# Attention and feed-forward on one core: attention steps of the last two blocks taken in pairs, weights and kept sums stored as pairs of parts

## The chip, the core and the metric

The kernel runs on one core of a Trainium2 chip. The metric is the device time of one execution in microseconds (us). A core has TensorE (PE in the rows; its weight loads are PEld), VectorE (DVE), ScalarE (ACT), GpSimd (POOL), and SyncE (SP), which here issues nearly all DMAs.

## What is computed

Windowed causal attention over 8 batches of 8 heads, 576 tokens, head size 64, then a feed-forward layer with a piecewise gate on all 4608 tokens:

```python
scores = scale * np.matmul(q, k.transpose(0, 1, 3, 2))
mask = (rel >= 0) & (rel < 64)                    # rel = query position - key position
attn = softmax(np.where(mask, scores, -1e9))
x = (attn @ v).transpose(0, 2, 1, 3).reshape(4608, 512)
h = x @ w_in                                      # 512 -> 2048
g = np.where(h >= 1, h, np.where(h <= -1, 0.0, (h + 1) ** 2 / 4))
out = g @ w_out                                   # 2048 -> 512
```

## The kernel before, in words

**Tiling.** Attention goes in 36 steps of 128 tokens, all heads in one step. A step has a scores part (`att_scores`: 64 matmul records of 96 columns for nearly all steps, S in what follows) and a values part (`att_values`: 32 records of 64 columns, V). The feed-forward layer works on tiles of 512 tokens with matmuls of 128x512. Every float32 operand of it is split into a high and a low part, and a product is three matmuls: high by high, high by low, low by high. I call the feed-forward matmuls dense.

**Stages.** Three tiles of 512 tokens go plainly (`add_ffn`, lines 1139 and 1185). The other six go as three blocks of 1024 tokens (`add_super`), in which seven products of halves take the place of eight. Its sums of weights are made once (`add_sums`) and kept in DRAM (`kept`); each group of 6 dense matmuls then reads one part of them through a ring of 7 buffers (`add_ring`, `ring_load`). The first layer of a block is line 914 (`ffn_product`), the second line 1000 (`out_product`). The attention of a block has 8 steps and runs inside the dense work of the block before it.

**Order.** No queue is filled by hand. Each piece of work is added to a list with a key, a cost for each engine that may do it, and what it waits for, takes and gives (`Plan.add`). `Plan.run` goes through the list with these costs, the free buffers and the keys, and writes each engine's instructions in the order in which it took them. The constants at the top (`A_SUPER`, `B_DUE`, `W_LATE`, ...) shift the keys or are costs. On the chip each engine then takes its instructions in that order, and waits on semaphores.

**One step from scores to values** (steps from 5 on): S into two banks of PSUM (`ps_a`); on DVE `att_masked` (line 445, 8 instructions of 128x96), on ACT `att_exp` (line 465, 8 activations), on DVE `att_inverse`, on DVE or POOL `att_normalize` (line 484), on DVE `att_turn` (line 491, a transpose in squares of 32). Then SP writes the result to a DRAM tile in two DMAs (`att_write`, `moved<-sm`) and reads it back transposed (`att_read`, `ptd<-moved`). There is one such DRAM tile and one buffer for the read (`pt2=1`), so a write waits for the read before it, and a read for the V that uses the buffer. V is followed by `x_take`, a copy out of PSUM on ACT or DVE (`raw<-ps_a`).

In the blocks `add_step` holds two steps open (`BEHIND = 2`). Each of the middle six steps gives PE one item: V of an older step, then S of the new one. The first two steps of a block are lone S, the last two V lone:

```python
            def do(e):
                if t < PLAIN:
                    att_scores(s, masked, ps)
                att_values(sv, pj)
                if t >= PLAIN:
                    att_scores(s, masked, ps)
```

**Start.** The first four steps add the mask by a matmul (line 415) and transpose on PE (`att_transpose_pe`, line 520), since the way over DRAM takes longer. Meanwhile the weights are loaded as 64-bit numbers (`raw<-in_w`) and made into high and low parts on ACT and DVE (`w_rest`, `w_top`, `w_join`, `w_high`, `w_low`; lines 328 to 344).

Of the kernel before, what the change touches and what calls it, by code (L numbers as in the profile page):

```python
# [10 lines left out]
F32 = mybir.dt.float32  # L11
# [9 lines left out]
P = 128  # L21
# [21 lines left out]
E_SPAN = 5.91  # L43
E_LEAD = 17.1
W_LEAD = -23.43
W_FIRST = (41.07, 11.15, 26.87, -10.88, -31.72)
W_STEP = 25.17
L_LEAD = -2.38
W_LATE = (3.63, -16.39, 9.21, 20.15, 0.56)
V_LATE = 14.51  # L50
W0_KEY = -103.61
FIRST_LOAD = 0, (0,)
M_LATE = 5.76
W0_STEP = 8.68
FINE = 4
NWARM = 8
A_FIRST = (-100.35, -96.85, -96.18, -80.14)
A_NEXT = 10.78
A_STEP = 5.01
A_SPAN = 18.65  # L60
A_LEAD = 5.32
O_LAG = 2.91
# [11 lines left out]
B_DUE = (4.53, -27.23, 1.18)  # L74
B_STEP = 13.93
B_FIRST = -15.42
A_END = 2.75
V_PE = 1270
NORM = dict(Pool=800, DVE=480), dict(DVE=610)
G_LATE = (11.92, 0.97, -5.01, 12.64, 1.72)  # L80
D_LATE = (-2.36, 0.62, 26.98, 2.89, 13.75, 21.44)
TURN = 965, 1500
# [4 lines left out]
SUM_KEEP = 880  # L87
V_LATE_2 = 43.01
LAND = 800
WRITE = 1140  # L90
BACKLOG = 2500
MOVED = 3700
PATIENCE = dict(ACT=300, DVE=0, Pool=303, PE=0, SP=0)
BUFS = dict(qt=2, kt=2, vt=4, ps_a=2, sm=2, ptd=3, pt2=1, x=2, u=2, ps_h=2, a=2, gh=2, gl=2, acc=4, o=2, tmp=2)
BUFS.update({n: 1 for n in ("xtmp", "xs0", "xs1", "xs2", "xs3", "xs4", "xs5", "X", "Y")}, raw=4, ring=7, op=5)

# [4 lines left out]
S_LATE = 5.22  # L101
S_PACE = 47.29
O_CHANGE = (-1.18, 7.84, 12.31)
EARLY_2 = 3.64
A_SUPER = ((10.49, 4.41), (12.01, 4.44))
A_ORDER = (0, 4, 1, 5, 2, 6, 3, 7)
BUILD = (-17.42, 29.27)
# [5 lines left out]
R_LEAD = -10.33  # L113
R_LOAD = 370
L_DVE = 4, 6, 8
G_LEAD = (9.32, -1.73, 0.08, 4.82)
OP_LEAD = 45.65
D_LEAD = 1.02
# [6 lines left out]
class Plan:  # L125
# [29 lines left out]
    def run(self):  # L155
# [22 lines left out]
        for _ in self.work:  # L178
            best = None
            for e in engines:  # L180
# [12 lines left out]
                if could:  # L193
                    until = min(could)[0] + PATIENCE[e]
                    c = min((c for c in could if c[0] <= until), key=lambda c: c[1:])
                    best = c if best is None else min(best, c)
# [26 lines left out]
def banded_attention_then_ffn(ctx: ExitStack, tc: tile.TileContext, q, k, v, w, masks, out, out_t, dims):  # L223
# [26 lines left out]
    idt = const.tile([P, P], F32, name="idt")  # L250
    make_identity(nc, idt)
    msk = const.tile([P, 3, WIN], F32, name="msk")
# [51 lines left out]
    ws, wts, zs, us = {}, {}, {}, {}  # L304
# [29 lines left out]
    def w_high(g, eng):  # L334
        f, units = g
        ws[g] = t = wpool.tile([P, len(units), 2, DM], F32R, name="wts", tag=f"w{f}_{units[0]}")
        for j, u in enumerate(units):
            wts[f, u] = t[:, j]
        us[g] = us[g].bitcast(F32).rearrange("p (u n) -> p u n", n=DM)
        copy(eng, t[:, :, 0], us[g])  # L340

    def w_low(g):
# [1070 lines left out]
```

## Time and profile before

| | |
|---|---|
| median of 3 runs | 836.71 us (836.44 to 837.24) |
| profiled execution | 835.11 us, its span 833.2 us |
| PE busy | 817.4 us, 98% of the span |
| DVE, ACT, POOL busy | 673.7, 520.8, 229.8 us |
| moved by DMA | 216.06 MB, 259 GB/s on the mean |

The span goes from the first instruction to the last. PE's busy time is the union of its matmuls, whose ends are modelled; where the text needs what a part really takes, it uses the distance from the start of one row to the start of the next. "[0.58 <-DMA ptd<-moved]" at the end of a row says that the engine sat idle for 0.58 us before it and what ended that.

### The profile page before, as it was taken

How to read it: one execution, taken by the hardware profiler on the slowest of the kernel's cores; microseconds unless marked ns; L12 is line 12 of the kernel's file. 1: busy time of each engine (PE TensorE's matmuls, PEld its weight loads, DVE VectorE, ACT ScalarE, POOL GpSimd, SP SyncE). 2: the span in 40 equal slices, each digit the busy share in tenths (PEclk: the TensorE clock that was granted, in tenths of full speed). 3: DMA queues.
4: the chain of work that ended last, by engine and by line, in shares of the span. 5: the costliest groups of instructions: out<-in, count | busy, mean ns of one | idle time of the engine just before them, and what ended most of it. 6: DMA issues, size and time to landing. Idle time of an engine off the chain costs nothing.

```text
span 833.2 us, 18542 instructions
## 1 busy us (share of the span) xinstructions
PE 817.4 (98%) x6588; PEld 670.0 (80%) x6588; DVE 673.7 (81%) x1551; ACT 520.8 (63%) x1287; POOL 229.8 (28%) x244
## 2 busy tenths in 40 slices
PE   5999999999999999999999999999999999999998
PEld 4778888888887888888888788888888888888886
DVE  6999976467765699599899995888999948888964
ACT  7889955555666656667875563777655535566442
POOL 1000043346645744556223321140133101100100
PEclk8999999999999999999999999999999999999999
DMA  9993389976778985899978979899787786666675
GB/s 350 421 418 107 103 273 358 358 241 207 220 254 267 286 258 159 285 313 341 332 221 278 311 240 341 276 293 311 221 240 230 251 252 193 193 194 194 202 218 162
DMA packets 151900, 216.06 MB, mean 259 GB/s; under 512 B 11905, under 2 KB 75265, under 8 KB 151809
## 3 DMA queue, kind: packets, MB, share of 16 engines
q1 hardware_dynamic: 151520, 213.97, 79.6%
q8 instruction: 52, 0.85, 0.4%
q10 hardware_dynamic: 288, 0.92, 0.3%
q14 instruction: 40, 0.32, 0.1%
HBM read 163.72 MB, written 51.12 MB: 258 GB/s over the span
## 4 chain that ended last, share of the span: by engine, by line
PE 87%; DMA 6%; DVE 5%; ACT 1%; issue 0%; SPq 0%; ACTq 0%; DVEq 0%
PE acc L1000 23%; PE acc L1185 14%; PE ps_h L1139 14%; PE ps_h L914 14%; PE acc L914 14%; PE ps_a L422 3%; DMA kt<-in_k 2%; PE ps_h L535 1%; PE acc L535 1%; PE ps_a L535 1%; DMA vt<-in_v 1%; DMA ptd<-moved 1%; DVE g L978 1%; DVE op L991 1%; DMA raw<-in_w 1%; DMA moved<-sm 1%
## 5 line engine op out<-in xcount | busy, mean ns | idle before, releaser
L1000 PE MATMUL acc<-op,wts 128*128 128x512 f32 x576 | 138.4, 391 | 0.0
L294 ACT CAST op<-g 128x512 fp32r<-128x512 f32 x125 | 77.7, 622 | 84.4 <-PE acc L1000 49.3
L1139 PE MATMUL ps_h<-xh,wts 128*128 128x512 f32 (+1 forms) x424 | 129.9, 373 | 0.0
L1000 PEld LDWEIGHTS acc<-op,wts 128*128 128x128 f32 x576 | 107.6, 188 | 22.9
L1185 PE MATMUL acc<-wts,gh 128*128 128x512 f32 x384 | 120.3, 395 | 0.0
L991 DVE TENSOR_TENSOR op<-g,op 128x512 fp32r<-128x512 f32 x119 | 87.6, 737 | 17.7 <-ACT op L294 17.0
L465 ACT ACTIVATE sm<-sm,nm 128x96 f32<-128x96 f32 x248 | 89.5, 363 | 14.3 <-DVE nm L445 12.5
L914 PE MATMUL ps_h<-wts 128*128 128x512 f32 x360 | 92.1, 391 | 0.0
L914 PE MATMUL acc<-wts 128*128 128x512 f32 x360 | 91.9, 390 | 0.0
L1139 PEld LDWEIGHTS ps_h<-xh,wts 128*128 128x128 f32 x424 | 77.5, 188 | 15.2 <-issue 0.3
L1185 PEld LDWEIGHTS acc<-wts,gh 128*128 128x128 f32 x384 | 70.7, 188 | 15.4
L1154 ACT ACTIVATE a<-a 128x512 f32<-128x512 f32 (+1 forms) x129 | 79.5, 617 | 3.9
L914 PEld LDWEIGHTS acc<-wts 128*128 128x128 f32 x360 | 67.4, 188 | 14.6 <-issue 0.3
L914 PEld LDWEIGHTS ps_h<-wts 128*128 128x128 f32 x360 | 67.2, 188 | 14.6
L1139 PE MATMUL ps_h<-xl,wts 128*128 128x512 f32 (+1 forms) x212 | 78.6, 371 | 0.0
L1185 PE MATMUL acc<-wts,gl 128*128 128x512 f32 x192 | 74.9, 390 | 0.0
L1149 ACT ACTIVATE a<-g 128x512 f32<-128x512 f32 x96 | 60.3, 629 | 19.9 <-DVE g L929 15.1
L1161 DVE SCALAR_TENSOR_TENSOR g<-a,g 128x512 f32<-128x512 f32 x96 | 67.9, 714 | 5.4 <-ACT a L1154 5.2
L1171 POOL TENSOR_TENSOR gl<-a,gh 128x512 fp32r<-128x512 f32 (+1 forms) x34 | 46.8, 1378 | 59.8 <-ACT gh L1166 55.0
L1149 ACT ACTIVATE a<-ps_h 128x512 f32<-128x512 f32 (+1 forms) x53 | 29.5, 557 | 53.4 <-PE ps_h L1139 53.0
L1161 DVE SCALAR_TENSOR_TENSOR a<-a,ps_h 128x512 f32<-128x512 f32 (+1 forms) x53 | 33.6, 634 | 34.8 <-ACT a L1154 34.5
L978 DVE TENSOR_TENSOR g<-g 128x512 f32<-128x512 f32 x82 | 56.9, 708 | 0.4
(142 smaller groups left out, 1529.4 us busy)
## 6 DMA issues: line engine op xcount, KB each, us to landing
wts<-kept SPq DMA_DIRECT2D x240, 256.0 KB, 3.5
vt<-in_v SPq DMA_DIRECT2D x72, 256.0 KB, 5.7
ptd<-moved SPq DMA_DIRECT2D x31, 512.0 KB, 4.6
kt<-in_k SPq DMA_DIRECT2D x35, 384.0 KB, 6.0
kept<-wts SPq DMA_DIRECT2D x48, 256.0 KB, 4.6
gh<-kept SPq DMA_DIRECT2D x48, 256.0 KB, 3.5
gl<-kept SPq DMA_DIRECT2D x48, 256.0 KB, 3.7
raw<-in_w SPq DMA_DIRECT2D x12, 1023.8 KB, 12.3
```

The costliest lines, as they stand in the source:

```text
L294: nc.scalar.copy(dst, src)
L465: nc.scalar.activation(t, t, AF.Exp, bias=nm[:, g:g + 1], scale=-1.0, accum_out=den[:, g:g + 1])
L914: nc.tensor.matmul(ps, lhsT=r[:, part, cp], rhs=x_op(k, xp)[:, cp], start=j in (0, 1, 3, 4) and i == 0 and cp == 0, stop=j in (1, 2, 5, 6) ...
L978: engine[eng].tensor_tensor(out=g[:, out], in0=g[:, a], in1=g[:, b], op=op)
L991: engine[eng].tensor_tensor(out=low, in0=g_of(n)[:, of], in1=high.bitcast(F32), op=ALU.subtract)
L1000: nc.tensor.matmul(opened[b][m], lhsT=r[:, part, m], rhs=op[xp], start=j in (0, 1, 3, 4) and i == 0 and n == 0, stop=j in (1, 2, 5, 6) and ...
L1139: nc.tensor.matmul(ps, lhsT=wts[f, 0][:, part, c * P:(c + 1) * P], rhs=x[:, c, r], start=(c == 0 and j == 0), stop=(c == NP - 1 and j == 2),)
L1149: nc.scalar.activation(gs[t, f, r.start][0], phs[t, f, r.start], AF.Relu, bias=0.5, scale=0.5)
L1154: nc.scalar.activation(a, a, AF.Square)
L1161: nc.vector.scalar_tensor_tensor(out=ps if t >= PLAIN else a, in0=a, scalar=1.0, in1=ps, op0=ALU.min, op1=ALU.max)
L1171: engine[eng].tensor_tensor(out=g[2], in0=g[0], in1=g[1].bitcast(F32), op=ALU.subtract)
L1185: nc.tensor.matmul(acc[t, i][:, n], lhsT=g[:, sub], rhs=wts[f, 1][:, part, n], start=(q == 0 and j == 0), stop=(q == NF - 1 and j == 2 and ...
```

## The change

1. **Pairs of steps.** In the last two blocks `add_pairs` takes the place of `add_step`. A block's 8 steps make 4 pairs and 5 runs on PE: S S, three times V V S S, V V. The first S of a pair takes two banks of `acc` or `ps_h`, the second two of `ps_a`, which it gets when both V before it have been copied out. A table `P_SHIFT` shifts each run, by the change's words so that borders of PE's instruction packets fall well.
2. **Two buffers for the read** (`pt2=2`): the old one, and two tiles in the room of the early masks and of `lent`, which was the ring's fifth buffer. The ring has 6 buffers instead of 7. The write still waits for the read before it, since the DRAM tile is still one.
3. **Weights as pairs of parts.** Weights lie as [chunk of 128][high, low][128] instead of [high, low][512]. Kept sums go to DRAM in one DMA of 1 KB packets where there were two of 512 B; the second layer's plain matmuls read their moving operand in 4 pieces of 128.
4. **POOL may do more**: `w_low`, the early `att_normalize`, and `ffn_low` of the first tile.
5. **Fewer waits in the plan**: the sums of `x_sums` and `g_sum` wait only for what they read.
6. **10 more matmul records in the warm-up**, and new values of nearly all constants, so that the order moves everywhere.

```diff
-TURN = 965, 1500
+TURN = 965, 100
-V_LATE_2 = 43.01
+V_LATE_2 = 63.45
+P_SHIFT = ((-0.59, -6.76, -5.83, 5.27, -24.12), (2, 5.54, 6, 4.47, -26.37))
...
+    def turned_of(b):
+        if b == 0:
+            return [turned[:, i] for i in range(2)]
+        if not spare:
+            spare.extend(const.tile([P, NP * SB], F32, name="ptd", tag=m) for m in ("lent", "early"))
+        return spare
...
-        x = add(key - W_LATE[4], dict(DVE=low), lambda e: w_low(g), [x], gives=[("u", xr)])
+        x = add(key - W_LATE[4], dict(DVE=low, Pool=200 + 2.15 * m), lambda e: w_low(g, e), [x], gives=[("u", xr)], shared=True)
...
+    def add_turn(s, xs, dk, banks, sm):
...
+        x = [add(due, dict(SP=HOP_SP[0]), lambda e, j=j: att_write(s, j), [x, *last["d"]], moves=packets(192, 1024, WRITE), gives=[sm] * j) for j in range(2)]
+        x = add(due, dict(SP=HOP_SP[1]), lambda e: att_read(s, x), x + last["t"] + early_values, takes=["pt2"], moves=packets(256, 2048))
+        last["d"] = last["t"] = [x]
+        return x
...
+    def add_pairs(u):
...
+            for j, (s, xt_, v) in enumerate(before):
+                after = [xs] if j else needs + [y for _, a, b in before for y in (a, *b)]
+                xs = add(
+                    now if j else key, dict(PE=V_RUN[j] + (150 if r == 4 and j else 0)), lambda e, s=s: att_values(s, "ps_a"), after,
+                    takes=["ps_a"] + room * (j == 0), gives=[("pt2", xt_), ("vt", v[0]), ("vt", v[1])],
+                )
...
+            x1 = add(
+                now if before else key, dict(PE=S_RUN[not before]), lambda e, s=steps[0], pj=pj: att_scores(s, False, pj), [xs] if before else needs,
+                takes=[] if before else room, gives=[("qt", q), ("kt", k)],
+            )
...
+            x2 = add(
+                now, dict(PE=S_RUN[2]), lambda e, s=steps[1]: att_scores(s, False, "ps_a"), [x1], takes=["ps_a", "ps_a"],
+                gives=[("qt", q), ("kt", k)],
+            )
...
     for u in range(SUPERS):
-        for i in A_ORDER:
-            add_step(PLAIN + 2 * u, i)
+        if u:
+            add_pairs(u)
+        else:
+            for i in A_ORDER:
+                add_step(PLAIN, i)
         add_super(u)
```

**What moves on PE, in the first layer of the first block** (L535 and L422 are V and S before, L564 and L435 after; L914 and L999 dense; a record count in the trace is twice the count of V and S here). Before:

```order
L914 MATMUL ps_h<-wts 128x512 x6
L535 MATMUL acc<-ptd,vt 64x64 x16
L422 MATMUL ps_a<-kt,qt 32x96 x32
L914 MATMUL acc<-wts 128x512 x6
L914 MATMUL ps_h<-wts 128x512 x6
L914 MATMUL acc<-wts 128x512 x6
L914 MATMUL ps_h<-wts,gh 128x512 x6
L914 MATMUL acc<-wts,gl 128x512 x6
L535 MATMUL acc<-ptd,vt 64x64 x16
L422 MATMUL ps_a<-kt,qt 32x96 x32
```

After:

```order
L999 MATMUL acc<-wts 128x512 x6
L564 MATMUL ps_a<-ptd,vt 64x64 x32
L435 MATMUL acc<-kt,qt 32x96 x32
L435 MATMUL ps_a<-kt,qt 32x96 x32
L999 MATMUL ps_h<-wts 128x512 x6
```

Two V and two S stand in one run. In the last two blocks 10 runs each become 5. Between the runs now stand 120, 108, 246 and 126 dense matmuls in the first of these blocks' attention, and 168, 186, 156 and 108 in the second's.

**On POOL at the start**, after the masks are made. Before:

```order
L273 MEMSET msk 64x64 x2
L494 MEMSET ptd 64x256
L828 TENSOR_TENSOR u<-wts 128x256 x2
L835 TENSOR_TENSOR u<-u 128x128 x4
```

After:

```order
L284 MEMSET early 64x64 x2
L357 TENSOR_TENSOR wts<-u,wts 128x4x128
L497 TENSOR_TENSOR sm<-sm,den 128x512 x3
L357 TENSOR_TENSOR wts<-u,wts 128x4x128
L497 TENSOR_TENSOR sm<-sm,den 128x512
L1256 TENSOR_TENSOR gl<-a,gh 128x256 x2
L357 TENSOR_TENSOR wts<-u,wts 128x8x128
L1256 TENSOR_TENSOR gl<-a,gh 128x256
L497 TENSOR_TENSOR sm<-sm,den 128x768
```

POOL takes 7 of the 20 weight subtractions (2 of 512, 5 of 1024 columns) and 5 of the 10 early normalizations, which DVE did.

**On SP, around a pair** of the second block's attention, in the change:

```order
L515 DMA moved<-sm 64x3x256 x2
L979 DMA gh<-kept_92 128x512
L979 DMA gl<-kept_93 128x512
L979 DMA wts<-kept_94 128x512
L533 DMA ptd<-moved 128x512 x2
L979 DMA wts<-kept_95 128x512
L979 DMA wts<-kept_94 128x512
L979 DMA wts<-kept_95 128x512
L515 DMA moved<-sm 64x3x256 x2
```

The second step's write stands behind the first step's read, with ring loads between them.

## Rows read from the trace of the kernel before

**Rows 1.** The page, DMA queues, PE's instructions: packets, MB, share of 16 engines.
```profile
q8 instruction: 52, 0.85, 0.4%
```

**Rows 2.** Busy time by stretch: length, PE, PEld, DVE, ACT, POOL, clock, DMA share, GB/s.
```profile
20.90:25.75 4.85, 4.85 (x106) 3.71 (x105) 4.78 (x11) 3.73 (x10) 0.00 (x0) 1.00 1.04 425
...
60.00:100.00 40.00, 40.00 (x293) 32.66 (x293) 38.93 (x67) 37.36 (x74) 0.30 (x1) 1.00 0.36 122
...
330.00:830.00 500.00, 498.99 (x3455) 409.59 (x3453) 421.19 (x883) 298.34 (x676) 113.24 (x99) 1.00 0.81 255
```

**Rows 3.** Waits of PE: who for whom, us in total, times, longest.
```profile
PE ps_a L422 <- DMA qt<-in_q: 2.2, 1, 2.2
...
PE ps_h L535 <- DMA ptd<-moved: 0.8, 1, 0.8
...
PE ps_a L535 <- DMA ptd<-moved: 0.6, 1, 0.6
```

**Rows 4.** Timeline of PE around a V with an S: start, length, instruction.
```profile
342.18 1.52 PE L914 MATMUL ps_h<-wts 128*128 128x512 f32 x6
343.63 1.15 PE L535 MATMUL acc<-ptd,vt 128*64 128x64 f32 x32
344.71 1.00 PE L422 MATMUL ps_a<-kt,qt 64*32 64x96 f32 x64
345.63 1.67 PE L914 MATMUL acc<-wts,gh 128*128 128x512 f32 x6
347.14 1.55 PE L914 MATMUL ps_h<-wts,gl 128*128 128x512 f32 x6
```

**Rows 5.** The same in the second layer: dense work after an S, then a lone V.
```profile
453.69 1.67 PE L1000 MATMUL acc<-op,gl 128*128 128x512 f32 x6
...
460.44 0.39 PE L1000 MATMUL acc<-gh,wts 128*128 128x512 f32 x1
460.76 1.15 PE L535 MATMUL ps_a<-ptd,vt 128*64 128x64 f32 x32
461.84 1.66 PE L1000 MATMUL acc<-op,wts 128*128 128x512 f32 x6
463.33 1.52 PE L1000 MATMUL acc<-op,gh 128*128 128x512 f32 x6
464.69 1.52 PE L1000 MATMUL acc<-op,gl 128*128 128x512 f32 x6
```

**Rows 6.** The same at the start.
```profile
1.46 3.78 PE L284 MATMUL acc<-ptd 128*128 128x128 f32 x16 [1.46 <-DVE ptd L278]
...
22.97 1.15 PE L535 MATMUL acc<-ptd,vt 128*64 128x64 f32 x32
24.05 0.73 PE L415 MATMUL acc<-mskr,idr 128*128 128x512 f32 x2
...
31.34 0.63 PE L520 MATMUL ps_a<-idt,sm 128*128 128x128 f32 x4 [0.58 <-DVE sm L484]
...
51.12 1.10 PE L422 MATMUL ps_a<-kt,qt 64*64 64x128 f32 x32 [0.46 <-DMA kt<-in_k]
```

**Rows 7.** Timeline of ACT: the copy out of PSUM after the lone V.
```profile
461.96 0.59 ACT L294 COPY raw<-ps_a 128x512 f32<-128x512 f32 x1 [0.42 <-PE ps_a L535]
```

**Rows 8.** Chain of waits, 440 to 485 us: turn, (write,) read, V.
```profile
467.94 0.89 DVE sm L491
...
472.45 5.08 DMA ptd<-moved
477.67 1.15 PE ps_a L535 x32
```

**Rows 9.** Groups by line and shape, 330 to 650 us: busy, mean ns, idle before.
```profile
L465 ACT ACTIVATE sm<-sm,nm 128x96 f32<-128x96 f32 x119 | 43.0, 363 | 9.1 <-DVE nm L445 8.5 <-POOL sm L484 0.6
```

**Rows 10.** DVE from 10 to 100 us, by line: busy, mean ns.
```profile
L344 DVE TENSOR_TENSOR wts<-u,wts 128x1024 fp32r<-128x1024 f32 (+1 forms) x17 | 17.1, 1013 | 0.4 <-ACT wts L294 0.4
...
L484 DVE TENSOR_TENSOR sm<-sm,den 128x512 f32<-128x512 f32 (+1 forms) x12 | 8.6, 728 | 0.0
```

More of the change, by code (lines that the diff above doesn't have):

```diff
@@ L630, in add_build @@
         i0 = add(due, tt(2 * SB), lambda e: x_sums(r, 0, e), [x0, x1], takes=["xtmp"] + ["u"] * first, shared=True)
-        xs = i0
-        for j in range(1, 4):
-            xs = add(due, tt(2 * SB), lambda e, j=j: x_sums(r, j, e), [xs], shared=True)
-        end = []
+        i2 = add(due, tt(2 * SB), lambda e: x_sums(r, 1, e), [i0], shared=True)
+        i1 = add(due, tt(2 * SB), lambda e: x_sums(r, 2, e), [i0], shared=True)
+        i3 = add(due, tt(2 * SB), lambda e: x_sums(r, 3, e), [i1], shared=True)
+        lows = []
         for k in range(6):
             n = 4 * SB if k == 0 else 2 * SB
-            after, slot, takes = [xs], f"xs{k}", []
+            after, slot, takes = [(i0, i1), (i2,), (i3,), (x0, x1), (x0, x1), (x0, x1)][k], f"xs{k}", []
+            after = list(after)
             if (u, k) in x_of:
@@ new lines, in add_loads @@
+    def add_loads(s, lk, vk, vc):
+        xq = add(lk, dict(SP=390), lambda e: load_q(s), takes=["qt"], moves=packets(P, 4 * DM))
+        xk = add(lk, dict(SP=480), lambda e: load_k(s) if s else None, takes=["kt"], moves=packets(P, 6 * DM) if s else None)
+        xv = add(vk, dict(SP=vc), lambda e: load_v(s, 0), takes=["vt"], moves=packets(P, 4 * DM), behind=last["v"])
+        xw = add(vk, dict(SP=vc), lambda e: load_v(s, 1), takes=["vt"], moves=packets(P, 4 * DM), behind=[xv])
+        last["v"] = [xw]
+        return xq, xk, xv, xw
@@ new lines, in add_take @@
+    def add_take(u, i, due, xo, pv):
+        s, r = starts[PLAIN + 2 * u] // SB + i, i % 4
+        after, takes = [xo], []
+        if i < 4:
+            takes = ["raw"]
+            if u == 0:
+                after.append(x_in[PLAIN - 2])
+        else:
+            after.append(raw_of[u, r])
+        x = add(due, dict(ACT=485, DVE=608), lambda e: x_take(s, i, e), after, takes=takes, gives=[(pv, xo)])
+        if i < 4:
+            raw_of[u, r] = x
+        else:
+            add_build(u, r, max(due, 0), raw_of[u, r], x)
@@ L1252, in add_gate @@
         xl = add(
-            key + late[4], low, lambda e: ffn_low(t, f, r, e), [xh], takes=["gl"], gives=[("a", xa)], shared=t > 0,
+            key + late[4], low, lambda e: ffn_low(t, f, r, e), [xh], takes=["gl"], gives=[("a", xa)], shared=True,
         )
```

301 lines of the change are left out of this document (167 added, 134 removed).

## Prediction

> **What bounds the kernel now.** Start with the table of stretches: from 330 to 830 us PE is busy for 498.99 of 500 us, and from 60 to 100 for all 40, at the full clock [rows 2]. So what other engines do there costs nothing as long as PE doesn't wait, and it hardly does: the waits of PE on the read after the turn are 0.8 and 0.6 us, once each, and the largest shown, 2.2, is that for the first queries [rows 3]. A time can fall in three ways: PE's own instructions take less, PE starts sooner, or these few waits go.
>
> Does PE work at full rate while busy? A group of 6 dense matmuls takes 464.69 - 463.33 = 1.36 us, 0.227 each [rows 5]. Around attention it is slower. Take a V with an S [rows 4] from start to start: the 6 ahead of it take 343.63 - 342.18 = 1.45 (0.09 over 1.36), V 1.08, S 0.92, the 6 behind 1.51 (0.15 over). So a run has **edges** of 0.24 us beside V and S. Around a lone V [rows 5] the matmul ahead takes 0.32 (0.09 over 0.227) and the 6 behind 1.49 (0.13 over): edges of 0.22. That is what pairs can save.
>
> **The change, part by part** (gain positive).
>
> *Fewer runs.* Each of the two blocks has 6 runs of V and S, 2 lone S, 2 lone V. With 0.24 for a run that ends in S and 0.22 for one that ends in V that is 8 x 0.24 + 2 x 0.22 = 2.36 us a block. After, it is 4 x 0.24 + 0.22 = 1.18. **Gain 2.4** for both. Elsewhere there are 29 runs where there were 28: **-0.2**.
>
> *Joints inside a run.* There will be 8 joints of V with V and 8 of S with S; no row has one. Below: V takes 1.08 us ahead of S [rows 4] and ahead of dense work [rows 5] alike, so it may take 1.08 ahead of V, and the joint gains 0. Above: a joint may save all that stands behind a part at an edge, 0.13 for V, 0.15 for S: 8 x 0.28 = 2.2. I take half, since V and S use the array in other shapes than dense work and have none to change at such a joint: **1.1**.
>
> *Second S waits for banks.* It needs the banks of both V, so the copy of the second must end while the first S (0.92 us) runs. After the lone V, which ended at 461.84, the copy ended at 461.96 + 0.59 = 462.55, 0.71 later [rows 5, 7]: in time. At worst another copy of 0.59 is ahead of it, and it is 0.4 late, or 0.6 behind something longer: 0 to 0.6, six times. I take 0.1: **-0.6** (0 to -3.6).
>
> *Old waits on the read.* 0.8 and 0.6 [rows 3]. With two buffers a read needn't wait for the V before; pairs move the later one. **1.2** (0 to 1.4).
>
> *New waits on the read.* The costliest unknown. The write of a pair's second step must wait until the read of the first has landed (SP's order: write, read, write). What a turn, write and read take is seen once where V waited for them: 477.67 - 467.94 = 9.73 us, of which the turn 0.89 and the read's landing 5.08 [rows 8]. Two in sequence, the second turn being done by then: 9.73 + 8.84 = 18.6 us. Ahead of this lie masks, exponentials, normalization, in DVE's queue. In the traced step S ended at 453.69 [rows 5] and the turn began at 467.94, 14.3 us later, behind other DVE work. The change orders fewer instructions ahead of most turns; what must be there needs about 5 (an estimate: 8 exponentials at 0.363 are 2.9 [rows 9]; a normalization of 768 columns by that of 512, 0.73 [rows 10], is 1.1; a mask and two short ones make up the rest). So from a run's end to the second V's data it is between 24 and 33 us. Available are the dense matmuls up to the run and its first V: 120, 108, 246, 126, 168, 186, 156, 108 at 0.227, plus 1.08: 28.3, 25.6, 56.9, 29.7, 39.2, 43.2, 36.4, 25.6. At 26.6 the two shortest are late by 1.0 each: **-2.0**, which I take as near the low end, since these turns have been given early places. At 24 it is 0; at 33 it is 4.7 + 7.4 + 3.3 + 7.4 = 22.8.
>
> *Start.* DVE is busy for 38.9 of 40 us from 60 to 100, POOL for 0.3, and for nothing in the earlier stretch shown [rows 2]. Moving 5 normalizations at 0.73 and 7 weight subtractions at 1.01 (means over both lengths) takes 10.7 us off DVE [rows 10]. PE's waits that hang on it: 0.58 in the third transpose, as an example; and 0.46 on keys, whose load now stands ahead of most weights on SP [rows 6]. That is 1.0 us shown, and I take **1.5**, as the 10.7 us lie on the engine that PE's first work waits for (3.5 if dense work also starts a third of them sooner, -2.5 if it starts later, since the third scores and the second V now stand ahead of it). The 10 more warm-up records, 3.78 / 16 = 0.24 each [rows 6], are 2.4 us, nearly inside the 2.2 us wait for the first queries [rows 3]: 0; if queries came at once, -2.4.
>
> *At nothing:* moving operands in 4 pieces. An early V reads 64 columns in a row, a later one 2 pieces of 32; 22.97 to 24.05 and 343.63 to 344.71 are 1.08 each [rows 4, 6]. Fewer, larger DMA packets of kept sums: no wait of PE on them is listed. One ring buffer less: 6 groups of 1.36 are 8.2 us ahead, and SP's issues keep their place; with that cover gone PE would wait at each group, which I hold for unlikely.
>
> **Sum:** 2.4 - 0.2 + 1.1 - 0.6 + 1.2 - 2.0 + 1.5 = **3.4 us**. The profiled execution of 835.11 (span 833.2, and 1.9 around it) would become 831.7. The median of the runs shown stands 1.6 above it, 836.71; from there I forecast **833.3**.
>
> **A rule to weigh: PE's instruction packets.** The queue for PE's instructions moved 52 packets of together 0.85 MB, 16 KB each; 0.4% of 16 engines' 833 us over 52 is 1.03 us a packet [rows 1]. An S issues its 64 matmuls with as many weight loads in 0.92 us [rows 4], so 256 instructions would last 1.84 us, longer than a packet's transfer. In before no V or S around a border is longer than the others. The Trainium skill (Runtime: NRT & Kernel Launch, Instruction fetch mechanics) says that instructions are fetched in blocks of 256 while the block before runs, and that the cost of crossing is mostly hidden. By that rule where a run stands among the borders changes nothing, and the sum stays at 3.4; the trace agrees so far, though none of its runs has more than half the instructions of a run of two V and two S.
>
> **Rivals.**
> *A, packets come too late in long runs.* Two V and two S are 384 instructions, with one or two borders. If the transfer were exposed at each of some 9 in six runs, 9 x 1.03 = 9.3: 842.6 us. Against: the 1.84 us above. For: never tried in before.
> *B, the second step's data is late* (slower). From a run's end to the second V's data 30 us instead of 26.6: late by 1.7, 4.4, 0.3 and 4.4, 10.8 in place of 2.0: 842.1. It decides at 28.3, where two waits of 2.7 eat the gain of 5.4. For: 33 by the traced step. Against: shorter queues ahead of these turns.
> *C, more than forecast:* the start gives 3.5 and no new wait comes: 833.3 - 2.0 - 2.0 = 829.3. For: POOL's idleness. Against: ACT, too, is busy for 37 of 40 us there.
> *D, the change doesn't do what it says:* joints cost as much as edges (no 2.4, no 1.1), the start gives what it gave, and no read is late: 3.4 - 3.5 - 1.5 + 2.0 = 0.4: 836.3, no change.
> *E, the clock falls in a run.* The granted clock stayed at 1.0 from 20.9 to 25.75, with nothing but attention on PE [rows 2], and a run of 3.8 us is shorter than that. Held for unlikely and put with A.
>
> **How the numbers follow.** Chances: forecast 0.45 (831 to 835.3, by the bounds of joints, banks and start), C 0.20, D 0.12, B 0.14, A with E 0.09. A measurement of this kernel tells 0.2%, 1.7 us, from no change, so faster means under 835.0, slower over 838.4. Faster: 0.42 of the forecast's, all of C, 0.02 of B with small lateness: 0.64. Same: 0.03 of the forecast's, D, 0.02 of B: 0.17. Slower: the rest of B and A: 0.19. For 8 in 10 the range reaches from 829.0, which leaves out half of C, to 838.5, which leaves out most of B and A.
>
> **What would show it.** Right: in the second and third blocks runs of about 1.08 + 1.0 + 0.8 + 0.92 with one pair of edges; the list of PE's waits has reads of 1 us or so at the two shortest distances; PE's dense work from 60 us on stands 1.5 us sooner. Wrong: reads waited for at more than four runs (B); gaps inside V or S at a PE fetch (A); a V or S as long as before with 0.2 to spare at each joint (D); first dense work late. The forecast fails as a whole if PE's idle time grows by over 4 us.

## The result and the profile after

The changed kernel took 845.03 us (median of 4 runs, 844.22 to 846.29), the kernel before 836.62 beside it (836.44 to 837.24): 1.0101 times as long, with an interval of 1.0083 to 1.0118. Forecast were 833.3 us and 829.0 to 838.5. The profiled execution took 845.14 us, its span is 842.3; that of before took 835.11, its span is 833.2. So the two spans differ by 9.1 us, about as much as the medians (8.4).

Busy time by stretch in the changed kernel, columns as in [rows 2]:

```profile
25.75:30.76 5.01, 2.67 (x26) 2.13 (x23) 4.56 (x12) 4.33 (x22) 2.27 (x2) 1.00 1.03 414
30.76:34.17 3.41, 3.41 (x41) 3.07 (x40) 1.78 (x5) 1.91 (x6) 1.04 (x1) 0.50 1.07 423
60.00:100.00 40.00, 40.00 (x403) 31.99 (x402) 35.90 (x70) 33.59 (x71) 15.60 (x9) 1.00 0.59 203
330.00:830.00 500.00, 493.96 (x3581) 404.83 (x3580) 411.44 (x902) 301.77 (x699) 89.26 (x85) 1.00 0.82 256
345.00:690.00 345.00, 338.96 (x2751) 276.72 (x2750) 290.38 (x679) 216.88 (x544) 73.44 (x71) 1.00 0.87 275
```

From 60 to 100 us POOL now works for 15.60 us and DVE for 3 us less, and PE is busy all the time, as before. From 330 to 830 PE is busy for 493.96 us where it was 498.99: 5 us of idle time are new, at full clock. The row of 30.76 has PE at half clock (0.50), as it also is from 13.60 to 20.40 (0.51; there in the kernel before, too, 0.50). Who is waited for, PE's waits in the changed kernel, columns as in [rows 3]:

```profile
PE ps_h L999 <- DMA wts<-kept: 1.9, 2, 1.2
...
PE ps_h L564 <- DMA ptd<-moved: 1.3, 2, 0.8
PE ps_a L548 <- POOL sm L497: 1.2, 1, 1.2
...
PE ps_a L564 <- DMA ptd<-moved: 1.1, 1, 1.1
PE ps_h L1224 <- DVE xl L577: 1.1, 1, 1.1
...
PE ps_h L999 <- DVE g L307: 0.9, 1, 0.9
...
PE acc L1085 <- DMA wts<-kept: 0.5, 2, 0.3
...
PE acc L999 <- DVE op L307: 0.5, 1, 0.5
PE ps_h L999 <- DMA gh<-kept: 0.5, 1, 0.5
PE ps_a L435 <- issue: 0.3, 1, 0.3
```

Five of these rows (and more like them that are left out) are dense matmuls that wait for a load of the ring (`wts`, `gh`, `gl` out of `kept`), or seem to wait for DVE there. Before, no such row was among PE's waits. The reads after the turn (L564) are waited for in the first block and ahead of it only, none in a run of pairs. PE's timeline in the changed kernel (start, length, instruction):

```profile
18.79 1.92 PE L435 MATMUL ps_a<-kt,qt 64*64 64x128 f32 x32
...
27.98 0.66 PE L548 MATMUL ps_a<-early,sm 128*128 128x128 f32 x4 [1.18 <-POOL sm L497]
28.39 0.36 PE L1224 MATMUL ps_h<-xh,wts 128*128 128x256 f32 x1
29.82 0.39 PE L1224 MATMUL ps_h<-xl,wts 128*128 128x256 f32 x1 [1.07 <-DVE xl L577]
...
349.92 1.62 PE L999 MATMUL ps_h<-wts 128*128 128x512 f32 x6 [0.87 <-DVE g L307]
...
382.54 1.63 PE L999 MATMUL ps_h<-wts 128*128 128x512 f32 x6 [1.16 <-DMA wts<-kept]
...
402.40 0.82 PE L435 MATMUL ps_a<-kt,qt 64*32 64x96 f32 x37
403.57 0.54 PE L435 MATMUL ps_a<-kt,qt 64*32 64x96 f32 x26 [0.35 <-issue]
...
461.04 2.09 PE L564 MATMUL ps_a<-ptd,vt 128*64 128x64 f32 x64
...
464.78 1.66 PE L1085 MATMUL acc<-op,wts 128*128 128x512 f32 x6
```

A run of V V S S lasts 464.78 - 461.04 = 3.74 us, where two runs of V and S took 2 x 2.00 [rows 4] and their edges twice. That is what was forecast. What was forecast wrongly are the start and the dense waits.

**Where the 9.05 us went.** PE's first instruction starts at 1.46 us in both profiles; its last ends 9.05 us later. I compared at which time PE has done the same amount of attention and dense work:

| stretch of the changed kernel | PE falls back by | of it |
|---|---|---|
| to 60 us | 2.9 | the start, the clock among it |
| 60 to 347 us | 1.0 | three new waits on reads, 1.12, 0.51 and 0.83 (186.79, 303.51, 304.68), one of 0.8 gone, the rest in small pieces of both signs |
| 347 us to the end | 5.15 | runs +1.67, edges +1.90, an old read's wait +0.61; 12 dense waits -8.55, a stop inside S -0.35, small pieces -0.43 |

The 12 waits are 5.66 us of idle time and 0.24 us more in each: the last matmul ahead of a wait takes 0.39 us where the next one otherwise starts after 0.227, and the first behind it takes 0.31. From 678 us to the end PE stays 9.05 us behind, so the plain tiles there, whose second layer now reads in 4 pieces, cost no more than before.

**What the dense waits hang on.** The end of the chain of waits of the changed kernel from 370 to 383 us (start, us, what), and SP's timeline there:

```profile
374.58 1.19 PE acc L999 x6
375.77 6.63 DMA wts<-kept
382.40 0.14 issue
382.54 0.47 PE ps_h L999
```

```profile
370.25 1.91 SPq L413 DMA_DIRECT2D vt<-in_v  x3
372.24 0.55 SPq L403 DMA_DIRECT2D qt<-in_q  x1
...
373.79 1.28 SPq L407 DMA_DIRECT2D kt<-in_k  x1
375.12 0.55 SPq L413 DMA_DIRECT2D vt<-in_v  x1
375.77 1.17 SPq L979 DMA_DIRECT2D wts<-kept  x2
```

A pair loads the inputs of two steps: 8 DMAs, 2.3 MB together, from 370.25 to 375.67 on SP. Behind them in SP's queue stands the ring's load. It is issued at 375.77 and lands 6.63 us later, with most of the 2.3 MB still in flight ahead of it (without such loads, below, a `wts` load lands in 3.8 us in the median, not in 4.2), and PE starts 0.14 us after that. All twelve waits end so, 0.13 us behind a ring load's landing, also the one at 349.92 that is put down to DVE.

Here is a second kind, SP's timeline from 622 us and the end of the chain. The read of a pair's first step (L533) goes out at 622.02. The write of its second step (L515) goes to the same DRAM tile, so it waits until that read has landed, and the ring's load behind it is issued late, at 628.20:

```profile
622.02 0.79 SPq L533 DMA_DIRECT2D ptd<-moved  x2
622.91 1.33 SPq L979 DMA_DIRECT2D wts<-kept  x3
626.86 1.24 SPq L515 DMA_DIRECT2D moved<-sm  x2
628.20 0.55 SPq L979 DMA_DIRECT2D gh<-kept  x1
...
628.20 4.09 DMA gh<-kept
...
632.42 0.47 PE acc L1085
```

Such writes wait for longer than before. SP's waits from 60 to 830 us, first in the kernel before, then in the changed one:

```profile
SPq L502 <- DMA ptd<-moved: 7.8, 5, 1.9
...
SPq L515 <- DMA ptd<-moved: 20.5, 12, 3.9
```

Of the twelve late ring loads six stand behind input loads, four behind a write that waits for a read, one behind a write that waits for its transpose on DVE, and one behind a read.

I call **time in hand** how long a ring load has been there when its group of matmuls starts. From 345 to 690 us it was 4.21 us in the median before (a tenth of the loads under 1.52), and 2.79 after (a tenth under 0.84). The DMA share is 0.87 in both.

### The profile page after: what moved, and what is told of

The parts are those of the page before. It is cut to its first block, busy times and chain, and to the rows that moved or that the text cites. A ratio compares the mean times of both kernels' runs of the same rounds, so it can differ in the third digit from the quotient of the medians.

```text
span 842.3 us, 18473 instructions
## 1 busy us (share of the span) xinstructions
PE 820.5 (97%) x6598; PEld 672.7 (80%) x6598; DVE 670.4 (80%) x1571; ACT 520.8 (62%) x1288; POOL 222.0 (26%) x223
## 4 chain that ended last, share of the span: by engine, by line
PE 86%; DMA 8%; ACT 2%; DVE 2%; SPq 1%; issue 1%; POOL 0%; ACTq 0%; POOLq 0%
PE acc L1085 25%; PE ps_h L1224 15%; PE acc L1270 14%; PE ps_h L999 12%; PE acc L999 12%; PE ps_a L564 3%; DMA wts<-kept 3%; PE ps_a L435 3%; DMA gh<-kept 1%; DMA moved<-sm 1%; PE ps_h L564 1%; DMA ptd<-moved 1%; DMA raw<-in_w 1%; DMA gl<-kept 1%; PE acc L435 1%
## 5 line engine op out<-in xcount | busy, mean ns | idle before, releaser
L1085 PE MATMUL acc<-op,wts 128*128 128x512 f32 x540 | 130.0, 390 | 0.3 <-DMA wts<-kept 0.3
L1085 PEld LDWEIGHTS acc<-op,wts 128*128 128x128 f32 x540 | 100.9, 188 | 22.7 <-issue 1.5
L1076 DVE TENSOR_TENSOR op<-g,op 128x512 fp32r<-128x512 f32 x119 | 83.0, 703 | 23.3 <-ACT op L305 22.3
L999 PE MATMUL ps_h<-wts 128*128 128x512 f32 x336 | 86.2, 392 | 3.0 <-DMA wts<-kept 1.9
L1239 ACT ACTIVATE a<-a 128x512 f32<-128x512 f32 (+1 forms) x138 | 85.4, 619 | 3.9
L999 PE MATMUL acc<-wts 128*128 128x512 f32 x336 | 85.4, 389 | 0.5 <-DVE op L307 0.5
L1234 ACT ACTIVATE a<-g 128x512 f32<-128x512 f32 x96 | 60.4, 629 | 33.7 <-DVE g L1014 27.7
L999 PEld LDWEIGHTS ps_h<-wts 128*128 128x128 f32 x336 | 62.4, 188 | 17.8 <-DVE g L1014 1.6
L999 PEld LDWEIGHTS acc<-wts 128*128 128x128 f32 x336 | 63.0, 188 | 14.0 <-DVE op L307 0.9
L1256 POOL TENSOR_TENSOR gl<-a,gh 128x512 fp32r<-128x512 f32 (+1 forms) x42 | 52.3, 1244 | 54.6 <-ACT gh L1251 49.8
L1063 POOL TENSOR_TENSOR g<-g 128x512 f32<-128x512 f32 x14 | 18.1, 1296 | 156.0 <-DVE op L1076 60.7
```

What stands on the lines that cost most here:

```text
L999: nc.tensor.matmul(ps, lhsT=r[:, part, cp], rhs=x_op(k, xp)[:, cp], start=j in (0, 1, 3, 4) and i == 0 and cp == 0, stop=j in (1, 2, 5, 6) ...
L1063: engine[eng].tensor_tensor(out=g[:, out], in0=g[:, a], in1=g[:, b], op=op)
L1076: engine[eng].tensor_tensor(out=low, in0=g_of(n)[:, of], in1=high.bitcast(F32), op=ALU.subtract)
L1085: nc.tensor.matmul(opened[b][m], lhsT=r[:, part, m], rhs=op[xp], start=j in (0, 1, 3, 4) and i == 0 and n == 0, stop=j in (1, 2, 5, 6) and ...
L1234: nc.scalar.activation(gs[t, f, r.start][0], phs[t, f, r.start], AF.Relu, bias=0.5, scale=0.5)
L1239: nc.scalar.activation(a, a, AF.Square)
```

## The experiments

Theory **R**: these waits are ring loads that come late, for two reasons. Pairs put lumps on SP, inputs and writes of two steps that stand together ahead of a ring load. And the ring gives less cover, the time from a buffer coming free to the group that needs its next load. Rivals: **D**, DVE or ACT are late with their operands, as some labels say; **P**, POOL's new work at the start slows what PE needs; and for the start its new order, or its copies and weights, each by itself. An edit called an order-edit lets the planner finish and then moves pieces in the list that it recorded, so that nothing else is planned anew:

```diff
-            do(e)
+            order.append((i, e))
...
+        for i, e in self.edit(order):
+            self.work[i][2](e)
```

### Which resource is late

**The inputs of later pairs left out.** All steps from 21 on, but for step 24, use tiles that an earlier step has loaded:

```diff
+    same = lambda s: s > 20 and s != 24
...
     def load_q(s):
+        if same(s):
+            qts[s] = held["q", s // 4 % 2]
+            return
```

> Leaves out a part: the queries, keys and values of the paired steps after the first pair aren't loaded, and these steps use the first pair's; 8 DMAs of 2.3 MB less after each of the six runs of V V S S. Order and ring (six buffers) as in the change. Theory L (pairs put the inputs of two steps in one row between ring loads; DMA and SyncE are held for 5 to 6 us, and the ring covers 6.8): the waits for ring loads after runs (2.6 us and four times 0.24 of filling) and the stall of 0.35 us for PE's instructions in the third run go: 845.0 - 4 = 841 us. Rival D (the waits hang on VectorE's and SyncE's order): 845, within 1, with ring loads no longer last but the same gaps.

837.04 us (835.6 to 840.15), before 836.08: 1.0014 (0.9994 to 1.0035). Its profile is of the longest of the five. PE's waits from 340 to 830 us, and the stretches:

```profile
PE ps_a L576 <- DMA ptd<-moved: 2.2, 2, 1.8
PE ps_a L447 <- issue: 0.8, 1, 0.8
PE acc L1097 <- DMA wts<-kept: 0.3, 1, 0.3
PE acc L1097 <- DMA gh<-kept: 0.2, 1, 0.2
```

```profile
25.75:30.76 5.01, 2.64 (x37) 2.13 (x32) 4.39 (x10) 4.32 (x22) 2.27 (x2) 1.00 1.04 416
30.76:34.17 3.41, 3.41 (x53) 3.21 (x52) 2.83 (x9) 2.88 (x10) 1.19 (x2) 1.00 1.06 423
345.00:690.00 345.00, 341.40 (x2766) 281.06 (x2765) 291.72 (x680) 216.72 (x536) 72.37 (x70) 1.00 0.76 230
```

With 230 GB/s moved in place of 275 the dense waits are down to half a us, and those on DVE are gone with them, though DVE is busy for as long (291.72 to 290.38). Up to the values of the last pair the last two blocks take 6.9 us less than in the change. There a new wait on a read stands, 1.83 us, behind which the granted clock is 0.52 from 670.0 to 673.5, and 3.7 us are lost again in this profile. The first two rows of stretches are taken up below, with the clock.

**Normalization in the last two blocks left out**, work of DVE and POOL:

```diff
     def att_normalize(s, h, eng):
+        if s >= 20:
+            return
```

> Leaves out a part: the normalization of the steps of the last two blocks (0.97 us on VectorE or 1.5 on POOL for each of 16 steps). Everything else as in the change. Theory D (the softmax ends of two steps stand in a row on VectorE ahead of the additions that free PE's banks, and their turns are late, with SyncE's queue waiting behind their writes): the waits that follow VectorE (0.87, 0.46, 0.28) and those behind a waiting write (0.26, 0.50, 0.51) go, with 0.24 each to fill: 845.0 - 4.3 = 840.7 us. Theory L: only the first three, 842.5, or no change where another VectorE instruction takes the place.

843.79 us (839.62 to 847.22): 1.0090 (1.0062 to 1.0118). Dense waits of 2.05, 0.82, 0.59, 0.53 and 0.50 us are still there. So the normalization isn't what PE waits for. With noloads, where DVE is as busy as in the change and the waits on it go, D falls.

**The seventh ring buffer back**, in the room of two early tiles; SP's order unchanged (order-edit):

```diff
+    aux = const.tile([P, DM], F32R, name="aux", tag="aux")
+    idr, mskr = aux[:, :P], aux[:, P:P + 2 * WIN].rearrange("p (a n) -> p a n", n=WIN)
...
+            elif i == 6:
+                ring_slots[i] = const.tile([P, DM], F32R, name="wts", tag="aux")
...
+            self.slots[i, "ring"] = [k % 7]
```

> The changed kernel with the order of every engine as it is, but with a seventh ring buffer (room for it is made of two tiles that are dead after the start). In the profiled execution of the change PE waits for ring loads at 382.5 (1.16 us), 413.3 (0.74), 473.5 (0.24), 491.7 (0.26), 569.5 (0.46), 632.4 (0.50) and 671.6 (0.51), 3.9 us, and each wait costs another 0.16 in which the array fills, together 5.0 us. Theory R (the ring is too short by one group of 1.36 us for loads that stand behind the inputs of two steps or behind a write that waits for the turn): all seven waits go, 845.0 - 5.0 = 840.0 us. Rival D (the groups are late because banks and evictions on VectorE are late, and the load is only what came last): nothing changes, 845.

845.18 us (841.77 to 849.31), before 836.83: 1.0107 (1.0074 to 1.0140). No gain in the end. The loads still stand where they stood on SP: a buffer comes free sooner, but the load is issued 0.92 us after that in the median, up to 6.9. The time in hand is 2.77 us, as in the change (2.79). The dense waits are 4.5 us of idle time in place of 5.66, and from 347 to 665 us PE gains 1.5 us on the change; but then it waits 2.37 us for the read of the last pair, with the granted clock at 0.50 behind it from 676.0 to 679.4, and 3.4 us are lost again. One of its rows shows who releases the wait that the change's profile puts down to DVE (349.92):

```profile
348.89 1.39 PE L1012 MATMUL ps_h<-wts 128*128 128x512 f32 x5 [1.14 <-DMA wts<-kept]
```

**The buffer, and each load moved ahead** (order-edit): seven buffers as above, and each ring load from the twelfth on takes the place of the one before it on SP.

```diff
+        at = [order.index(x) for x in loads[10:]]
+        for p, x in zip(at, loads[11:] + [None]):
+            order[p] = x
...
+        order.insert(at[0], loads[10])
```

> The change with seven ring buffers, and from the tenth on each ring load stands on SyncE where the load before it stood: so a load is issued one group, 1.36 us, sooner, also when inputs or a waiting write come behind it. In the change a ring load reaches its group with 2.8 us in hand at the median, 0.8 at the tenth percentile and nothing at ten groups, whose waits are 0.1 to 1.2 us. Theory R (the cover that the seventh buffer gave decides): all these waits but traces go, 5.3 us and ten times 0.24: 845.0 - 7.5 = 837.5 us. Rival B (the transfers themselves are late since the DMA engines are full; sooner issues only queue): slack grows by less than 0.7 us, and the time stays over 842; reads of the last pair may come later still.

840.15 us (837.49 to 842.72), before 836.52: 1.0047 (1.0025 to 1.0069); the profiled one is the shortest. Time in hand 3.95 us (a tenth under 1.55), nearly that of before. PE's waits from 340 to 830 us:

```profile
PE ps_h L1017 <- DMA wts<-kept: 2.0, 1, 2.0
PE ps_a L451 <- issue: 1.7, 1, 1.7
PE ps_a L580 <- DMA ptd<-moved: 1.5, 1, 1.5
PE ps_h L1017 <- DMA gh<-kept: 0.3, 1, 0.3
```

Two dense waits are left of twelve. That is R's doing: as many bytes at about the same rate (280 GB/s, in the change 275) and about the same landing time (4.1 us in the median, in the change 4.2), only issued sooner. It is the best version with pairs that does the whole work, 4.9 us under the change, and still slower than before.

**The pairs undone.** The last two blocks take single steps again; six buffers and all else stay, planned anew:

```diff
-A_SUPER = ((14.96, -42.48), (-9.45, -6.24))
+A_SUPER = ((14.96, -42.48), (12.01, 4.44))
...
-        if u:
-            add_pairs(u)
-        else:
-            for i in A_ORDER:
-                add_step(PLAIN, i)
+        for i in A_ORDER:
+            add_step(PLAIN + 2 * u, i)
```

> The change with its pairs undone: the last two blocks go by single steps again as the first block does (with the spacing of the kernel before), the order planned anew; start, six ring buffers, two buffers for the read, weights' layout and all other constants stay. If pairs as such are what costs (theories L and D: 8.9 us of new waits in the last two blocks against 3.9 us of saved edges and joints), the dense waits there fall under 2 us and the time is 845.0 + 3.9 - 7 = 842. Rival C (six buffers and the constants cost, not the pairs): the waits stay and the saved edges come back: 849.

853.73 us (852.83 to 856.15): 1.0213 (1.0192 to 1.0235). By its time it says little, since the new plan makes a wait of its own. PE's waits from 340 to 830 us:

```profile
PE acc L999 <- ACT o L305: 12.8, 1, 12.8
PE acc L999 <- DVE g L1014: 0.9, 1, 0.9
```

The 12.8 us (at 353.59) are a copy that waits for DMAs which stand on SP behind two writes and two reads; around it the granted clock is 0.50, from 342 to 359 us. After it, one wait of 0.9 is left, with six buffers (it, too, ends 0.13 us behind a ring load's landing): at 359 us PE is 18.2 us behind the kernel before, at 678 us 18.16. So **a ring of six with single steps loses nothing, a ring of six with pairs loses some 5 us net**. The buffer alone was not the fault; the time in hand here is 3.59 us.

**The inputs paced** (order-edits). Each input load of the later steps goes behind a ring load, one at a time (spread); or only queries and keys, behind every third (pace), and that with seven buffers (pace7):

```diff
+            if w in ("load_q", "load_k", "load_v") and s > 20 and s != 24:
+                later.append((i, e))
+                continue
+            out.append((i, e))
+            if w == "ring_load" and later:
+                out.append(later.pop(0))
```
```diff
+            if w in ("load_q", "load_k") and s > 20 and s != 24:
...
+            if w == "ring_load" and later and n % 3 == 0:
```

> The changed kernel with six ring buffers and one thing moved: the loads of queries, keys and values of a pair, which stand in rows of 4 to 8 on SyncE right after a run, are spread, one behind each ring load. Theory R1 (the ring starves because up to 2.3 MB of inputs of two steps go out in one row between two ring loads): the four waits that follow such rows (382.5, 413.3, 473.5, 569.5: 2.6 us, and 0.16 for each) go, 845.0 - 3.2 = 841.8 us. Rival R2 (it is the ring's length alone; the inputs only shift who is late): the same bytes meet other ring loads, the waits move and the time stays at 845, within 1.

> The change with one thing moved: of the row of loads after a run the four of values stay where they are, and the two of queries and two of keys (1.3 MB) follow one behind each third ring load. In the run where all eight were spread one behind each ring load, the ring starved for longer (waits of 24 us in all). Theory L (what counts is bytes between two ring loads: in 4.1 us now three ring loads and one of inputs, 1.07 MB, about 265 GB/s, where 420 is the most seen): the waits after runs fall from 2.6 us to under 1, 842.5 us. Rival (the later loads meet reads and writes of the pair or come late for the next run): no gain, or slower by some us, with PE waiting for queries or keys.

> The same with a seventh ring buffer. In the run with seven buffers alone the last two blocks gained 2 us up to 665 us and lost 3.6 in the last pair, whose second read landed in 7.2 us and made PE wait 2.4. Theory L: both together leave hardly a wait for ring loads, 839 us, and with more loads in flight at the last pair perhaps a wait of 2 for its read, 841. Rival: as with one of the two, 843 to 845.

859.56 us (1.0267, 1.0251 to 1.0283), 847.91 (1.0138, 1.0112 to 1.0165) and 847.31 (1.0141, 1.0125 to 1.0156). All three miss. In spread the dense waits grow to 14.2 us of idle time, some 24 us with what follows them, and the time in hand falls to 2.32 us. An input load put behind each ring load stands ahead of the next one; I take it that many loads are then late by one DMA where a few were late by eight. A lump moved is no lump removed: what helped was more lead for the ring (ahead7) or less to load (noloads).

### The start

**POOL's new work undone** (order-edit): early normalizations and weight subtractions on DVE.

```diff
+        dve = lambda w, s: w == "w_low" or w == "att_normalize" and s < 5
+        order = [(i, "DVE" if e == "Pool" and dve(*self.what(i)) else e) for i, e in order]
```

> The changed kernel in its own order, but the weight subtractions and the early normalizations that POOL does are done by VectorE, at the places where they stand in the order. Theory P (POOL's slower normalizations, 1.04 us against 0.6, make the transposes of step 0 and 2 late: PE waits 0.9 and 1.2 us for them): 1 to 1.5 us less, 843.7. Theory O (the order of the start, with the third scores at the half clock ahead of the first values, is what costs): within 0.7 of 845. If POOL's relief was worth what I forecast (1.5 us), it becomes 846.5.

845.61 us (842.58 to 848.12): 1.0095 (1.0071 to 1.0119). PE is 1.0 us later at 60 to 150 us than in the change, the time is the same. P falls: POOL's help is worth 1 us there, not a loss.

**The old order at the start** (order-edits): the first 300, 150 or 255 pieces as the kernel before has them, then the change's; with 255 also on top of ahead7.

```diff
+        order = first + [x for x in order if x[0] not in dict(first)]
```

> The changed kernel whose first 300 pieces of work (to about 75 us) are taken in the order and on the engines of the kernel before, POOL's new work among them undone; everything after stands in the change's order, and the warm-up stays 10 records longer. At equal progress of PE's work the change is 2.9 us behind the kernel before from 47 us on. Theory S (the start's new order costs 2.9 us): 845.0 - 2.9 = 842.1 us, the first dense matmul at 25.8 us instead of 28.4. Rival W (the longer warm-up or other weights' layout is what makes it late): the first dense matmul stays late by over 1 us and the time over 844.

> Like the run with 300 pieces of the earlier start, but only the first 150 (to about 38 us) in the order and on the engines of the kernel before. In that run the start was 2.8 us sooner at 70 us, as theory S says, and then PE lost 11.7 us where the two orders meet (81 to 96 us: scores and values of later steps taken ahead of their data). With the shorter piece the 2.6 us gained by 38 us should stay: 842.4 us. If the seam costs again, the gain up to 60 us tells alone.

> The change with its first 255 pieces of work (to about 65 us) in the order and on the engines of the kernel before. After 255 pieces both orders have done the same work but for two pieces on each side, so no seam as in the runs with 300 and 150. Theory S (the order of the start, of SyncE's loads above all, costs 2.8 us): 845.0 - 2.8 = 842.2 us, and 2.8 us less at 70 us of the profile. Rival: what is gained at the start is lost again to late loads by 200 us: 845.

> Both: the earlier start in its older order and the ring of seven with its loads one place ahead, pairs as in the change. If both theories hold: 845.0 - 2.8 - 7.5 = 834.7 us, 1 to 2 us under the kernel before, which is what pairs would be worth with nothing given back. If the last pair's read or the stall for PE's instructions in the third run takes 2 us: 837.

853.42 us (1.0199, 1.0173 to 1.0224), 850.90 (1.0181, 1.0156 to 1.0206), 845.70 (1.0128, 1.0104 to 1.0152) and 842.93 (1.0096, 1.0075 to 1.0117). Each won back what the start had lost, and lost more at the seam, where the two orders meet. With 300 pieces PE's progress equals that of before within 0.1 us up to 77 us, though warm-up and layout of the weights are the change's: these cost nothing. PE is 2.8 us ahead of the change at 70 us, then loses 11.7 at 81 to 96. With 255: 2.75 ahead, then 5.5 lost at 69 to 80, a stretch at half clock among it. With 150: 2.06 ahead at 38 us, then 7.0 of waiting for keys. The order is what costs the start 2.9 us; a kernel with the old start and the pairs, planned as one, wasn't tried.

**PE's order alone** (order-edit): six pieces are moved, among them the scores of step 2 behind the first V and the first two dense groups ahead of the third transpose; and that with pace and seven buffers (both).

```diff
+        for i, x in (47, 20), (41, 40), (42, 41), (68, 42), (283, 68), (297, 283):
...
+            order.insert([y[0] for y in order].index(x) + 1, a)
```

> The change with six pieces of work moved in the first 35 us: the values of step 0 ahead of the third scores, those of step 1 ahead of the fourth, its rounding ahead of the maxima of step 3, and the first two dense groups ahead of the transposes of step 2, as before; POOL keeps its new work. Theory O (the order costs 2.9 us, and POOL's relief gives back 1.0 of what it would cost): the first dense matmul at about 26 us instead of 28.4, and 845.0 - 2.5 = 842.5 us. Rival P (POOL's normalizations and the late maxima set the start whatever the order): within 1 of 845.

> Earlier start, paced loads and seven ring buffers together. If the parts add: 845 - 2.5 - 5 = 837.5 us, about the kernel before; if the stall for PE's instructions in the third run and the last pair's read stay or grow, 840.

849.40 us (845.92 to 852.08; 1.0159, 1.0137 to 1.0181) and 852.32 (850.76 to 856.67; 1.0211, 1.0187 to 1.0236). A miss: the first V now waits for copies on ACT (1.55 and 2.4 us in all), the transposes 1.5. PE runs at half clock for 10.2 us, as long as in the change in all, but here without a break. ACT's and SP's orders fit the change's order of PE, and a part of it can't be taken alone.

### Stops between instruction packets

The stop of 0.35 us at 403.57 lies 332 instructions into a run of 384. Counted through the program, that run alone of the six has two borders of 256 instructions in it. In all fifteen kernels that keep the pairs and the change's warm-up the same run stops at this place, for 0.35 us here up to 2.58 (start255). The kernel ahead7 with 25 matmuls of 2 columns in the warm-up, and 8 whole ones, has every later instruction of PE 80 places further on, so that five runs hold two borders; with 55 and 8 by 200 places:

```diff
+        for _ in range(25):
+            nc.tensor.matmul(ps[:, :2], lhsT=ptd[0][:, 0], rhs=ptd[0][:, 0, :2], start=True, stop=True)
...
-        warm(NWARM + 5)
+        warm(8)
```

> The version with seven buffers and loads one place ahead (840.2 us), whose warm-up now has 8 matmuls of 128 columns and 25 of 2 columns instead of 13 of 128: 80 PE instructions more ahead of everything. Counted by 256, the third run has one border then and no stop, but five other runs of V V S S have two borders, at 99 and 355, 112 and 368, 69 and 325, 58 and 314, 109 and 365 instructions of 384. Theory A (a packet isn't there yet when a second border comes within 2 us of the first): the stop of 1.7 us in the third run is gone, and the five runs stop before their last 15 to 35 records for 0.3 to 2.5 us each: 840.2 - 1.9 + 5 x 1.2 = 844. Rival (the stop hangs on this run's place, inputs or banks): it stays where it is, 840.

> The same with 55 matmuls of 2 columns: 200 PE instructions more, by which no run has two borders inside. Theory A: no stop in any run, 840.2 - 1.9 = 838.3 us, unless the longer warm-up (47 more matmuls) comes into the way of the first scores and takes 1 to 3 us back. Rival: the stop stays, 840.

848.32 us (845.48 to 849.55; 1.0125, 1.0103 to 1.0147) and 862.29 (860.58 to 864.19; 1.0300, 1.0276 to 1.0323). The second's warm-up takes some 18 us itself, so its time says nothing, but no S in it stops. In pad80 five stop, and where they should:

```profile
378.29 0.40 PE L453 MATMUL ps_a<-kt,qt 64*32 64x96 f32 x15 [1.06 <-issue]
...
468.26 0.37 PE L453 MATMUL ps_a<-kt,qt 64*32 64x96 f32 x8 [1.09 <-issue]
...
563.29 0.56 PE L453 MATMUL ps_a<-kt,qt 64*32 64x96 f32 x30 [1.28 <-issue]
```

Two more runs stop for 0.47 and 1.12 us: 5.0 us in all. The third run, where the change stopped, keeps 0.23. So a run with one border pays a quarter of a us at most, and one with two pays 0.47 to 1.28 here, 0.35 to 2.58 in the other kernels. Why the price differs so much stays open.

## Why the prediction was wrong

Its terms against what was measured:

| term | forecast | measured |
|---|---|---|
| fewer runs and joints | 2.4 - 0.2 + 1.1 = 3.3 | 3.6 (1.67 inside the runs, 1.90 at edges) |
| second S waits for banks | -0.6 | 0 |
| old reads | +1.2 | -1.1 (1.4 gone, 2.5 new, ahead of the pairs) |
| reads in pairs | -2.0 | 0 |
| start | +1.5 | -2.9 |
| ring with a buffer less | 0 | -8.55 |
| border inside a run | 0 | -0.35 |

Measured, these make -9.3 where PE fell back by 9.05; the rest is small pieces of both signs.

**Right:** runs. V V S S takes 3.73 to 3.82 us, edges 0.09 ahead and 0.13 behind (forecast 0.24 in all), and no S waits for its banks. So rival D falls. The way from a run's end to its second V's data took 27.7 us behind the first run (340.6 to 368.3), 26.8 behind the second (372.9 to 399.7) and 26.3 behind the last but one (648.7 to 675.0), forecast 26.6. That no read of a pair was waited for is partly the dense waits' doing: they gave the reads more time. Where the dense waits were taken away, the last pair's read was late: by 1.83 us (noloads), 1.5 (ahead7) and, with the ring but partly relieved, 2.4 (seven). The term of -2.0 is owed, in other words, and hidden; B had the right place and too high a price.

**The step that failed** is in "At nothing": "One ring buffer less: 6 groups of 1.36 are 8.2 us ahead, and SP's issues keep their place; with that cover gone PE would wait at each group, which I hold for unlikely." Neither half held. SP's issues did not keep their place among the others: pairs put two steps' inputs and their writes in front of a ring load, which made it 1.2 to 3.6 us late, and then it took 4.1 to 6.6 us to land. The 8.2 us are what seven buffers gave, six ahead of the one in use; six buffers have five ahead, 5 x 1.36 = 6.8 us, so that 1.2 + 4.1 fits and 1.2 + 6.6 doesn't. My own term for new waits had the second step's write wait for the first step's read; I asked what that does to V, and not what it does to the ring loads that stand behind the write on SP. And PE does not wait at each group or at none, but at those whose loads stand behind a lump: 12 of them, 8.55 us, more than all that the pairs saved. Neither cause does it alone: unpaired has six buffers and no such loss, seven has seven buffers and most of the waits. Noloads and ahead7 show the cause from both sides: less ahead of the ring loads, or the ring loads sooner, and most of the waits go. I had costed the cover by its length, and not by what of it was left: [rows 4, 5] gave the group's 1.36 us, but I took no row of a ring load's landing, 4.3 us in the median before. By 4.3 of 6.8 it would have stood as a rival.

**The other step** is the start, "**1.5**, as the 10.7 us lie on the engine that PE's first work waits for". I took what DVE gives away for a gain of PE, and my rows of PE's waits left out the largest of the kernel before, on the first transposes (16.54 us):

```profile
PE ps_h L520 <- DVE den L476: 4.0, 1, 4.0
```

The change begins them at 14.90 us, behind waits of 1.18 and 0.90; but so does nopool, at 15.02, with the work back on DVE, so this comes with the order and not from POOL. And the order of the first 60 us cost more than that: the scores of step 2 stand ahead of the first V, at half clock (18.79, 1.92 us), the third transpose waits 1.18 us for the very normalization that went to POOL, and the first dense group waits 1.07 us for `xl`. First dense work comes at 28.39, before at 25.75. Of the 2.9 us about 1.1 are the clock: after 5.01 us in which PE worked for 2.67, it was granted 0.50 from 30.76 to 34.17. The end of my own range there, -2.5 "if it starts later", was the better value.

**Rivals.** A was half right: a border may stop a run, but not each one, and by 0.35 us in the change, up to 1.28 in pad80. The Trainium skill (Runtime: NRT & Kernel Launch, Instruction fetch mechanics) says that a crossing is mostly hidden. The traces agree for one border in a run; with two they do not, 5 us in pad80. Two borders there are 256 instructions apart, some 2.3 us by the timeline. E holds in another place: the clock fell at the start, behind waits; from 330 to 830 us, with all runs of pairs, it stayed at 1.00. Why the times of the change spread (844.2 to 846.3, and its variants more) is shown in part: nine profiles have this start, and the stretch after 30.76 is at half clock in five and at full clock in four, with nearly the same work of PE ahead of it (2.67 us here; at full clock 2.64 in noloads and 2.68 in ahead7). Where it is at full clock PE is 1.1 to 1.3 us sooner than in the change, as the start of the sixth scores shows (47.32 us there). What decides between the two, and the rest of the spread, stays open.

## What to carry to other kernels

Merging runs saves what the edges show, but it also lumps the loads behind them: before a buffer is taken from a prefetch ring, list how long each load had been there when it was used, and count what the issuing queue will put ahead of it. Here a buffer more gave nothing by itself, and 4.9 us once its loads also moved ahead in that queue. A wait's label names the event that came last by the profile; look whether a DMA landed 0.1 us before it.

## What was unexpected

A wait costs more than its idle time, 0.24 us more here. Two packet borders within one run of 384 instructions stopped PE for 0.35 to 2.6 us, over all kernels tried. Matmuls of 2 columns in the warm-up of pad200 started 0.11 us apart at full clock, those of 128 columns ahead of them 0.21. PE then went on with matmuls of 2 columns without a break from 5.04 to 25.26 us, and yet its clock was 0.50 from 8.9 us on, where they started 0.21 us apart.
